# Two edits at the start of an attention and gated-MLP kernel: a limit on loads under way, and wider weights for the first block's projections

## The chip, the cores and the metric

The kernel runs on one core of a Trainium2 chip. The metric is the device time of one execution in microseconds, the median of several runs. TensorE multiplies matrices into PSUM, VectorE (DVE) and ScalarE (ACT) work on elements, GpSimd (POOL) does a few elementwise sums, and SyncE (SP) issues nearly all transfers between HBM and SBUF. PE stands for TensorE's matmuls and PEld for its weight loads.

## The reference

Two stages follow each other. The first is linear attention with random features, for 8 batches, 8 heads, 576 tokens and 64 channels a head:

```python
def phi(x):
    proj = np.einsum('bhsd,md->bhsm', x, omega)      # 64 channels -> 128 features
    sq = np.sum(x * x, axis=-1, keepdims=True) / 2.0
    h = proj - sq
    h = h - np.max(h, axis=-1, keepdims=True)
    return np.exp(h) / np.sqrt(m)
q_p, k_p = phi(q * scale), phi(k * scale)
kv = np.einsum('bhsm,bhsd->bhmd', k_p, v)
out = (q_p @ kv) / (q_p @ k_p.sum(2) + 1e-6)
```

The second takes the result as 4608 tokens of 512 channels and computes `((x @ w_a) * (x @ w_b)) @ w_out` with 1536 inner channels. All is float32.

## The kernel before

**Blocks and pairs.** A block is one batch. Two heads form a pair, their 64 channels each filling 128 partitions, so a block has four pairs (`NHP`). The attention of block 0 runs first; that of later blocks is woven into the MLP of the block before. The MLP splits its float32 operands into two float32r parts and runs three products for each, in `moe_block` (L1307 and the output product L1120) for the first blocks and in a seven-product scheme in `moe_block7` (L1405) for the rest.

**Order.** Every operation is an entry of a graph (`g.op`). The long list `ORDER` fixes in which order they are emitted, so each engine's instructions stand in a fixed order; an engine that waits holds up all that is behind it. Neither the list nor the slots of the buffers are touched by the change.

**Projections.** `four` (L576 and on) projects 512 columns of k and q of a pair: for each of 4 chunks of 128 tokens, 2 halves `t` of 64 tokens and 2 heads `w`, one matmul (L587) with 64 rows by 64 columns of X as weights and the 128 columns of omega streaming. That makes 16 matmuls, each of which shows as two rows of the trace (two passes of float32). The results stand in two PSUM tiles, `ppk` and `ppq`, one for each head row group. After it `scores` takes maxima on DVE (L659), biases (L666 to L673) and the exponentials on ACT (L680). Block 0 calls `four` nine times: twice for each of its four pairs, and once (`Xe`, tiles `ppke` and `ppqe`) for the last 64 tokens of all heads. Later blocks call it too, and `eight` (L607) has the same loop.

**Loads.** The helper `dma` (L406 and L407) issues a transfer on SP's queue. In the order of issue the first thirty are: X in two halves, ident, Xe, X, nat, then from the seventh X, v, nat, X, v, nat, raw (w_out), raw, raw, v, raw, raw, raw (w_out), natee, natk, v, v, X, raw (w_out), raw, natq, raw, natkk, raw. X holds transposed k and q of a pair, nat the same untransposed for the sums of squares (squared on POOL L750 or ACT L566, summed on DVE L752 or L571), v the values, raw weights of the MLP as they come from HBM. `om` (omega) is loaded by ACT's queue. A load takes its place in SBUF from a ring of buffers and waits until the old content is no longer read.

Of the kernel before, what the change touches and what calls it, by code (L numbers as in the profile page):

```python
# [17 lines left out]
P = 128  # L18
B, H, S, D, M = 8, 8, 576, 64, 128
# [177 lines left out]
    at=(  # L197
        "0123456705613412652106537451673260731742751346507163014510110101010101101010100101011010101001010101101001010101010101010101010110101010101010101010101010010101"
        "01010101010101010101010101010101010101010101"),
# [20 lines left out]
    w="345610287a9b",  # L220
    x="01230123012301230110",
    ab="01010101010101010101010101010101010101010101010101011001",
    a="101010101010101010101010",
# [15 lines left out]
    t=(  # L239
        "1230421341023401234102340123401234012340123401234012340123401234012340123401234012340123401234012340123401234012340123401234012340123401234012340123401234012340"  # L240
        "12340123"),
# [3 lines left out]
    c="021021021021021021021021021021021021021021021021021021021021021021021021021021021021",  # L245
# [110 lines left out]
def tile_attention_moe(ctx: ExitStack, tc: tile.TileContext, kqt, kqtt, kqn, kqnt, vx, omst, idn, wab, wout, out):  # L356
    nc = tc.nc
# [7 lines left out]
    def f(ap):  # L365
        return ap.bitcast(F32)

    g = Graph()
    for name, n in dict(X=2, Xw=0, natw=0, nat=2, x2=0, v=2, hk=1, hq=2, qd=1, kvz=0, sm=3, sq=3, ht=3, Xt=1, xl=0, xts=2, rd=2, x=4, xa=2, xf=2, Sa=2, Sb=2, st=0,
                        w=NF, u=NF, t=0, tst=0, wo=3, raw=2, a=2, c=0, bq=0, ghl=2, osb=0, ot=0, owr=0, og=0, ogf=0, oc=0, zs=1, z2=1, zb=2, k2=2, kl=1, dn=1, tails=0, zq=2, zx=2,  # L370
                        at=CFG["AT"], ab=2, o=4).items():
# [31 lines left out]
    def subber(o, i, hi):  # L403
        return lambda e: ENG[e].tensor_tensor(o(), i(), f(hi()), op=ALU.subtract)

    def dma(dst, src):  # L406
        return lambda e: nc.sync.dma_start(dst(), src())  # L407


    ident = fixed([P, P], F32, "ident")  # L410
# [20 lines left out]
    if CFG["IDSP"]:  # L431
        g.op({"SP": 450}, dma(lambda: ident.ap[:], lambda: idn), w=[(ident, None)], prio=-1396.5, nbytes=65536)
    else:
        g.op({"ACT": 60}, lambda e: nc.scalar.dma_start(ident.ap[:], idn), w=[(ident, None)], prio=-5000, nbytes=65536)
# [35 lines left out]
    for n, (kind, i, w) in enumerate(units):  # L470
        pr = 4000 + n * 4000 / len(units)
        more = late[:10] if n < 18 else late[:6] if n < 24 else late[:3] if n < 30 else late[:1] if n < 33 else []
        raw = g.buf("raw", [P, NW], I64 if wide else F32, f"raw{n}", more)
        src = (wab[i, w] if kind == "ab" else wout[i])
        g.op({"SP": 450}, dma(lambda raw=raw: raw.ap[:], lambda src=src: src), w=[(raw, None)], alloc=[raw], prio=pr - 600,
             nbytes=P * NW * (8 if wide else 4))
        if kind == "ab":
            hb = wab_b[i, w] = g.buf("wu"[i % 2], [P, 2, NC4, P], F32R, f"w{'ab'[w]}{i}")
            v = lambda hb, k: hb.ap[:, k].rearrange("p c f -> p (c f)")
        else:  # L480
            hb = wo_b[i] = g.buf("wo", [P, 2, E], F32R, f"wo{i}")
            v = lambda hb, k: hb.ap[:, k]
        convert(raw, lambda hb=hb, v=v: v(hb, 0), lambda hb=hb, v=v: v(hb, 1), hb, NW, pr, CFG["CONV"][0] + n * CFG["CONV"][1], n < NF)
        if kind == "o":
            db = g.buf(None, None, None, f"wod{i}")
            wo_store[i] = db
            g.op({"SP": 450}, dma(lambda i=i: wod[i], lambda hb=hb: f(hb.ap)), r=[(hb, None)], w=[(db, None)], prio=pr + 600,
                 nbytes=P * 2 * E * 4)
# [87 lines left out]
    def four(nm, b, pri, x, xdep, dst, c0, sm, sq, al, deps, mg, more):  # L576

        pps = [g.buf("at", [P, 4 * M], F32, f"pp{'kq'[w]}{nm}{c0}", more) for w in range(2)]
        plain = b == 0 and sq is not None
        mo = om2 if plain else om  # L580

        def go(e):
            for c in range(4):
                for t in range(2):
                    for w in range(2):
                        rows, half = slice(D * w, D * w + D), slice(D * t, D * t + D)
                        nc.tensor.matmul(pps[w].ap[half, c * M:c * M + M], x()[rows, c * P + D * t:c * P + D * t + D], mo.ap[rows], start=True, stop=True)  # L587
        lead = g.op({"PE": 940}, go, r=[*xdep, (mo, None)], w=[(pp, "p") for pp in pps], alloc=[*pps, *al], prio=pri, deps=deps, margin=mg, mode="r")
        flat = [lambda pp=pp: pp.ap for pp in pps]
        scores(nm, b, pri, x, xdep, dst, c0, sm, sq, flat, [[(pp, "p")] for pp in pps], more, plain)  # L590
        return lead
# [1040 lines left out]
```

## Time and profile before

| | |
|---|---|
| median of 3 runs | 1031.1 us (1031.01 to 1032.39) |
| the profiled execution | 1031.69 us |
| its span, first to last instruction | 1029.7 us |
| PE busy | 1021.7 us, 99% of the span, 9963 matmul rows |
| PEld busy | 900.4 us, 87% |
| DVE, ACT, POOL busy | 789.8 us, 637.8 us, 110.8 us |
| DMA | 312.95 MB, 304 GB/s over the span |

Busy time counts each engine's own instructions; a matmul's row includes its way through the array, so rows that follow closely overlap. About 2 us of the profiled execution lie outside the span.

### The profile page before, as it was taken

The numbers are of one execution on the slowest core, as the hardware profiler recorded it, in microseconds if no ns is written. First come the engines' busy times: TensorE is split into PE (matmuls) and PEld (weight loads), VectorE is DVE, ScalarE is ACT, GpSimd is POOL, SyncE is SP. The second block draws the span as 40 slices with busy tenths as digits, with TensorE's granted clock in tenths as the row PEclk, the third lists the DMA queues.
The fourth block names the chain that finished last, engine by engine and source line by source line (L and its number), as shares of the span: only waits on it lengthen the run. The fifth ranks groups of instructions, "written<-read, shape, count | busy, mean of one in ns | idle before, by whom it ended". The sixth has DMA issues, their size and how long they took to land.

```text
span 1029.7 us, 25658 instructions
## 1 busy us (share of the span) xinstructions
PE 1021.7 (99%) x9963; PEld 900.4 (87%) x9963; DVE 789.8 (77%) x1561; ACT 637.8 (62%) x1688; POOL 110.8 (11%) x182
## 2 busy tenths in 40 slices
PE   9999999999999999999999999999999999999998
PEld 7777777778788889888889988888888999999998
DVE  7999999999987877776767767687756467877555
ACT  7999998776676666675666556675654134344322
POOL 2012111210111111111110011111110000000000
PEclk9999999999999999999999999999999999999999
DMA  9787888998999999989898998989797888989981
GB/s 355 244 308 255 274 257 281 328 320 285 338 338 321 340 350 333 341 299 324 286 341 306 325 290 284 350 273 320 242 331 244 307 281 329 366 319 346 358 310 60
DMA packets 122185, 312.95 MB, mean 304 GB/s; under 512 B 17488, under 2 KB 39120, under 8 KB 122064
## 3 DMA queue, kind: packets, MB, share of 16 engines
q1 hardware_dynamic: 121600, 310.72, 87.6%
q8 instruction: 79, 1.29, 0.5%
q10 hardware_dynamic: 464, 0.59, 0.2%
q14 instruction: 42, 0.34, 0.1%
HBM read 254.74 MB, written 56.52 MB: 302 GB/s over the span
## 4 chain that ended last, share of the span: by engine, by line
PE 96%; DVE 3%; ACT 0%; issue 0%; DVEq 0%; ACTq 0%
PE p L1405 41%; PE o L1120 23%; PE pb L1307 6%; PE pa L1307 6%; PE o_P L1190 5%; PE pkv L906 3%; PE pm L977 2%; PE ppk L607 2%; PE ppk L587 2%; PE p L607 1%; PE p L1190 1%; DVE sm L659 1%; PE ppke L587 1%; DVE raw L456 0%; PE none L426 0%; DVE sq L752 0%
## 5 line engine op out<-in xcount | busy, mean ns | idle before, releaser
L1120 PE MATMUL o<-wo,ghl 128*128 128x512 f32 x1008 | 269.6, 397 | 0.0
L1120 PEld LDWEIGHTS o<-wo,ghl 128*128 128x128 f32 x1008 | 178.6, 188 | 35.5 <-issue 4.3
L396 ACT COPY c<-p 128x512 f32<-128x512 f32 x150 | 87.5, 583 | 182.0 <-PE p L1405 174.4
L1417 DVE TENSOR_TENSOR c<-p,c 128x512 f32<-128x512 f32 x144 | 98.7, 685 | 63.8 <-PE p L1405 36.5
L1405 PE MATMUL p<-Sa,t 128*128 128x256 f32 x1008 | 133.9, 282 | 0.0
L1405 PEld LDWEIGHTS p<-Sa,t 128*128 128x128 f32 x1008 | 126.9, 190 | 2.4 <-issue 0.3
L859 POOL TENSOR_TENSOR z<-hk 128x256 f32<-128x256 f32 x54 | 47.2, 873 | 610.5 <-ACT hk L627 356.1
L1481 DVE TENSOR_TENSOR c<-c 128x512 f32<-128x512 f32 x82 | 56.7, 696 | 46.3 <-ACT c L396 45.7
L1307 PE MATMUL pa<-x,wa 128*128 128x512 f32 x288 | 79.6, 400 | 0.0
L941 ACT ACTIVATE hq<-hq,dn 128x128 f32<-128x128 f32 x216 | 70.5, 393 | 11.9 <-DVE dn L937 11.5
L1307 PE MATMUL pb<-x,wb 128*128 128x512 f32 x288 | 77.8, 397 | 0.0
L1405 PE MATMUL p<-x,wb 128*128 128x256 f32 x504 | 73.5, 281 | 0.0
L1405 PE MATMUL p<-x,wa 128*128 128x256 f32 x504 | 73.4, 281 | 0.0
L1405 PEld LDWEIGHTS p<-x,wa 128*128 128x128 f32 x504 | 67.7, 189 | 2.9
L1405 PE MATMUL p<-Sb,bq 128*128 128x256 f32 x504 | 67.7, 283 | 0.0
L1405 PE MATMUL p<-x,t 128*128 128x256 f32 x504 | 67.5, 282 | 0.0
L1405 PEld LDWEIGHTS p<-Sb,bq 128*128 128x128 f32 x504 | 64.9, 189 | 2.9
L1405 PEld LDWEIGHTS p<-x,t 128*128 128x128 f32 x504 | 64.7, 189 | 2.9
L1405 PE MATMUL p<-Sb,t 128*128 128x256 f32 x504 | 67.0, 282 | 0.0
L1405 PEld LDWEIGHTS p<-x,wb 128*128 128x128 f32 x504 | 65.6, 189 | 0.1
L1405 PEld LDWEIGHTS p<-Sb,t 128*128 128x128 f32 x504 | 63.4, 189 | 1.4 <-ACT c L396 0.5
L1307 PEld LDWEIGHTS pb<-x,wb 128*128 128x128 f32 x288 | 53.3, 188 | 12.7 <-issue 0.9
(225 smaller groups left out, 1969.2 us busy)
## 6 DMA issues: line engine op xcount, KB each, us to landing
t<-td SPq DMA_DIRECT2D x168, 512.0 KB
wo<-wod SPq DMA_DIRECT2D x96, 512.0 KB
bq<-bd SPq DMA_DIRECT2D x84, 256.0 KB
qdr<-qd SPq DMA_DIRECT2D x108, 160.0 KB
hq<-qdr SPq DMA_DIRECT2D x27, 640.0 KB
X<-in_kqt_dram SPq DMA_DIRECT2D x30, 512.0 KB
raw<-in_wab_dram SPq DMA_DIRECT2D x24, 512.0 KB
td<-ts SPq DMA_DIRECT2D x24, 512.0 KB
```

What stands on the lines that cost most here:

```text
L396: nc.scalar.copy(o(), i())
L587: nc.tensor.matmul(pps[w].ap[half, c * M:c * M + M], x()[rows, c * P + D * t:c * P + D * t + D], mo.ap[rows], start=True, stop=True)
L607: nc.tensor.matmul(flat[c // 4][w]()[half, c % 4 * M:c % 4 * M + M], x()[rows, c * P + D * t:c * P + D * t + D], om.ap[rows], start=True, ...
L859: g.op({"POOL": pool2(n)}, lambda e: nc.gpsimd.tensor_tensor(o(), a(), c(), op=ALU.add), r=r, w=w, alloc=list(al), prio=pri, deps=zload[-1 ...
L906: nc.tensor.matmul(pkv.ap[D * j + d:D * j + d + Q, 0:M], vb.ap[:, vc, d:d + Q], c(), start=(n == 0), stop=(n == 4))
L941: g.op({"ACT": 392}, lambda e, c=c, src=src: nc.scalar.activation(hq.ap[:, c], src(), AF.Copy, scale=dn.ap[:, c:c + 1]), r=[sd, (dn, None) ...
L1120: nc.tensor.matmul(po.ap[:], ghl.ap[:, gi, t * P:(t + 1) * P], wo.ap[:, wi], start=(n == 0 and i == 0), stop=(n == NF - 1 and i == 2))
L1190: nc.tensor.matmul(pb.ap[:, t], A[0](ai)[:, t * P:(t + 1) * P], W[0](wi), start=begin and t == j == 0, stop=stop and j == 2 and (t == 1 or ...
L1307: nc.tensor.matmul(pb.ap[:], wt.ap[:, wi, c], xs[c].at(xi), start=(c == 0 and i == 0), stop=(c == NC4 - 1 and i == 2))
L1405: nc.tensor.matmul(pb.ap[:, w], W[w][0](wi, c), X[0](xi, c), start=fresh and n == w == 0, stop=n == 5, skip_group_check=True)
L1417: g.op({"DVE": dve(SM)}, lambda e: nc.vector.tensor_tensor(o.ap[:, q], pb.ap[:], C[y[0]].ap[:, y[1]], op=ALU.add), r=[(pb, 0), (pb, 1), (C ...
L1481: g.op({"DVE": dve(SM)}, lambda e, c=C[k]: nc.vector.tensor_tensor(c.ap[:, :, 1], c.ap[:, :, 1], c.ap[:, :, 0], op=ALU.mult), r=part, w=pa ...
```

## The change

The helper keeps a list of the loads it has issued. From the seventh to the thirtieth, each load waits until the third load before it has landed. In `four`, block 0 takes all 128 tokens of a chunk as the weights of one matmul (64 rows by 128 columns) in place of two matmuls with 64 columns each; for other blocks the loop stays. The matmul's output then fills all 128 partitions of its PSUM tile at once.

```diff
+    loads = []
+
     def dma(dst, src):
-        return lambda e: nc.sync.dma_start(dst(), src())
+
+        def go(e):
+            loads.append(nc.sync.dma_start(dst(), src()).ins)
+            n = len(loads) - 1
+            if 6 <= n < 30:
+                tc.add_manual_dep(loads[n], loads[n - 3].name, mybir.DependencyInfo(mybir.DependencyClass.Sync, mybir.DependencyReason.DATA), reason="few transfers at a time")
+        return go
...
             for c in range(4):
-                for t in range(2):
+                for t in range(2) if b else (None,):
                     for w in range(2):
-                        rows, half = slice(D * w, D * w + D), slice(D * t, D * t + D)
-                        nc.tensor.matmul(pps[w].ap[half, c * M:c * M + M], x()[rows, c * P + D * t:c * P + D * t + D], mo.ap[rows], start=True, stop=True)
+                        rows, half = slice(D * w, D * w + D), slice(0, P) if t is None else slice(D * t, D * t + D)
+                        nc.tensor.matmul(pps[w].ap[half, c * M:c * M + M], x()[rows, c * P + half.start:c * P + half.stop], mo.ap[rows], start=True, stop=True)
```

## Rows read from the trace of the kernel before

**Rows 1.** Busy time by stretch: engine busy us (instructions), granted clock, DMA share, GB/s.
```profile
0.00:50.00 50.00, 46.86 (x821) 37.01 (x822) 43.61 (x112) 41.75 (x126) 7.57 (x20) 1.00 0.81 299
50.00:1015.00 965.00, 964.96 (x9063) 853.71 (x9062) 738.48 (x1435) 595.37 (x1562) 103.20 (x162) 1.00 0.90 308
```

**Rows 2.** The same view, 10 to 50 us, with the sum over its stretches.
```profile
10.00:20.00 10.00, 8.84 (x208) 6.90 (x201) 9.83 (x22) 9.54 (x36) 5.35 (x6) 1.00 1.03 404
20.00:30.00 10.00, 9.70 (x224) 8.41 (x221) 9.73 (x32) 9.57 (x34) 0.20 (x1) 1.00 1.04 401
...
sum 40.00, PE 37.66 PEld 30.44 DVE 39.08 ACT 37.51 POOL 6.28; mean PE 9.42 PEld 7.61 DVE 9.77 ACT 9.38 POOL 1.57
```

**Rows 3.** Chain that ended last, 0 to 120 us: start us, us, what.
```profile
10.56 1.28 DVE sme L659 x2
...
27.45 0.59 DVE sqe L571
...
50.34 2.06 PE pb L1307 x9
```

**Rows 4.** Timeline of DVE: start, us, instruction, idle before and releaser.
```profile
3.72 0.69 DVE L643 TENSOR_TENSOR x<-X 128x512 f32<-128x512 f32 x1 [3.72 <-DMA X<-in_kqt_dram]
5.99 0.69 DVE L659 TENSOR_REDUCE sm<-ppq 128x4 f32<-128x512 f32 x1 [1.58 <-PE ppq L587]
...
9.88 0.68 DVE L659 TENSOR_REDUCE sm<-ppk 128x4 f32<-128x512 f32 x1
10.55 0.69 DVE L659 TENSOR_REDUCE sme<-ppke 128x4 f32<-128x512 f32 x1
```

**Rows 5.** Timeline of PE, warm-up and first projections.
```profile
0.78 3.15 PE L426 MATMUL none<-const-bfloat16-1.0 128*128 128x512 bf16 x7 [0.78 <-PEq L1616]
...
4.18 0.42 PE L587 MATMUL ppk<-om,X 64*64 64x128 f32 x1
...
4.39 0.42 PE L587 MATMUL ppk<-om,X 64*64 64x128 f32 x1
...
6.53 0.27 PE L587 MATMUL ppk<-om,X 64*64 64x128 f32 x1
...
6.64 0.27 PE L587 MATMUL ppk<-om,X 64*64 64x128 f32 x1
```

**Rows 6.** Weight loads grouped by line and shape: busy us, mean ns.
```profile
L1405 PEld LDWEIGHTS p<-Sa,t 128*128 128x128 f32 x1008 | 126.9, 190 | 2.4 <-issue 0.3
...
L587 PEld LDWEIGHTS ppk<-om,X 64*64 64x64 f32 x368 | 21.7, 139 | 7.0 <-issue 2.7 <-DMA om<-in_omst_dram 0.9 <-ACT wb L396 0.4
```

**Rows 7.** Timeline of SP, the queue of loads.
```profile
0.75 0.87 SPq L407 DMA_DIRECT2D X<-in_kqt_dram  x2
...
7.61 0.35 SPq L407 DMA_DIRECT2D raw<-in_wout_dram  x1
9.89 1.66 SPq L407 DMA_DIRECT2D raw<-in_wab_dram  x2
...
17.38 0.33 SPq L407 DMA_DIRECT2D natee<-in_kqnt_dram  x1
...
24.62 0.38 SPq L407 DMA_DIRECT2D raw<-in_wab_dram  x1
```

**Rows 8.** Timeline of POOL: the squares that wait for nat.
```profile
10.01 2.04 POOL L750 TENSOR_TENSOR nat<-nat 128x512 f32<-128x512 f32 x2 [4.88 <-DMA nat<-in_kqn_dram]
...
17.43 1.04 POOL L750 TENSOR_TENSOR nat<-nat 128x512 f32<-128x512 f32 x1 [2.42 <-DMA nat<-in_kqn_dram]
```

**Rows 9.** Timelines of ACT and of PE: first readers of late loads.
```profile
26.55 0.75 ACT L566 ACTIVATE natee<-natee 128x512 f32<-128x512 f32 x1
...
28.99 0.80 ACT L566 ACTIVATE natk<-natk 128x512 f32<-128x512 f32 x1
...
32.94 0.69 PE L1040 MATMUL pkv<-v,hk 128*64 128x66 f32 x16
```

**Rows 10.** Who waited for whom on SP, 0 to 45 us: us, times, longest.
```profile
SPq L407 <- DVE sq L571: 9.1, 1, 9.1
```

## The prediction

> **What bounds the kernel now.** I read the busy time by stretch first. From 50 to 1015 us PE is busy 964.96 of 965 us, while in the first 50 us it is busy 46.86 [rows 1]. Both edits act before about 40 us: the nine projections of block 0 and the loads up to the thirtieth. So whatever they do reaches the end only as a shift of the moment at which PE's solid stretch begins, and the shift arrives there undiminished. It is not multiplied either, since the order of each engine is fixed.
>
> Next comes the chain of waits in that first part. It passes from PE's projections to DVE with the maxima of `sme` at 10.56, stays mostly there (the sum `sqe` at 27.45 is one piece), and from 50.34 it is PE alone [rows 3]. DVE is busy 39.08 of the 40 us from 10 to 50, ACT 37.51, PE 37.66 [rows 2]. Hence the first part is bound by DVE, which has 0.92 us of idle time there in all. DVE's dense run begins at 5.99, when the first projection has ended, after 1.58 us of waiting for it [rows 4].
>
> The loads are the third thing to look at. DMA moves 404 and 401 GB/s from 10 to 30 us, its engines busy throughout [rows 2]. SP issues without a long pause until the thirteenth load at 7.61, and the next one only at 9.89; POOL gets the first nat, the sixth load, at 10.01. The same pairing returns at 17.38, where SP issues natee, the twentieth, and at 17.43, where POOL gets the last nat, the twelfth [rows 7, 8]. So today a load waits for the eighth before it: eight are under way, and the queue of transfers never runs dry.
>
> **The projections, part by part.** A call of `four` makes 4 chunks x 2 passes = 8 groups. A group is now four rows (two halves, two heads) that run in four quarters of the array at once. From group to group it takes 4.39 - 4.18 = 0.21 us early on, and 6.64 - 6.53 = 0.11 us later [rows 5]. The same work at twice the speed is the array's clock at its lower level (1.2 GHz), which it has up to about 6.5 us, and then at 2.4 GHz; PE multiplies from 0.78 on, first in seven matmuls of a warm-up [rows 5], and without a long break up to the rise. Because the group's time halves with the clock, it is set by the array and not by how fast instructions are issued.
>
> After the change a group is two rows, one a head, each with 128 columns of weights. The streams stay 128 columns long and the groups stay eight a call. What goes is half of the instructions, 16 x 9 = 144 matmul rows and as many weight loads, and by the argument above these are not what a group waits for. So I expect no gain from them. What can grow is the weight load: 139 ns for 64 columns and 190 ns for 128 [rows 6], some 51 ns more for 64 columns, so about 0.10 us for loading 128. That fits just under a stream of 0.11. The nearest row with 128 columns of weights is the MLP's product: 9 matmuls in 2.06 us are 0.229 each, while 512 columns at 2.4 GHz are 0.213, so each loses 0.016 [rows 3]. I take this 0.016 for each group: 8 x 0.016 = 0.13 a call.
>
> Four calls stand on the path before DVE's work at 10.55 (two halves of the first pair, one of the second, Xe): 4 x 0.13 = 0.5 us, less the 0.07 for which DVE waits there anyway (9.88 + 0.60 = 10.48, a 512-column maximum being issued every 0.6 us) [rows 4]. That makes **+0.45 us at 10.55**. The other five calls (+0.65 us of PE time) stand beside the DVE run, in PE's 2.3 us that are idle from 10 to 50 [rows 2]; without that cover they would be added. The lower end is 0, since a stream is not shortened. The upper end is a load that is not hidden at all, which is the first rival.
>
> **The limit on loads, part by part.** It removes nothing that is waited for: transfers start in the same order, DMA is already full, and a load cannot land earlier because fewer stand behind it. What it adds is a wait on SP. Everything behind it on SP's queue waits too, but that is again loads, in the same order, up to the thirtieth.
>
> The question is whether three loads are enough to keep the transfers dense. A single load of 256 KB, issued at 0.75, reaches DVE at 3.72 [rows 4, 7]: 2.97 us, of which 0.65 are its bytes at 404 GB/s and 2.32 the way there and back. A load of 512 KB needs 1.30 us for its bytes and one of 330 KB 0.84. With the limit, a load lands at the earliest 2.32 us plus its own bytes after the third before it; in a dense queue it lands after the bytes of three.
> - Three of 512 KB: 3.89 dense against 2.32 + 1.30 = 3.62. Nothing is lost.
> - Two of 512 and one of 330 KB, the last of 512: 3.43 against 3.62, a loss of 0.19. This happens at the ninth, the twelfth and the seventeenth load: 0.56 by natee, the twentieth.
> - From natk on (wout, natee, natk: 2.60 against 2.97; then natee, natk, v: 2.14 against 3.16) another 1.0, so that the v, X and weight loads up to the thirtieth come 1.5 to 1.8 us later.
>
> Who notices? natee: the eighteenth load lands when SP goes on at 24.62 with the twenty-sixth, then come 1.30 for w_out and 0.65 for natee, together 26.57. ACT squares natee at 26.55 without a pause before it [rows 7, 9]. So natee has no slack, and behind ACT's square waits `sqe` on DVE, a piece of the chain [rows 3]. natk, then due at 27.2 + 0.9 = 28.1, is read at 28.99, and the fourth v, due at 28.0 + 1.6 = 29.6, at 32.94 [rows 9]: both in time. The last loads find a cover too: SP stood 9.1 us waiting for DVE's `sq` to release a buffer [rows 10], and a delay of 1.8 is swallowed there. So the limit costs **0.5 us through natee**, between 0 (if the first load's way there and back was longer than a later one's by 0.3 us, all triples fit but the last, which nobody notices) and 2.6 to 3.3 (if all 2.97 us are the way there and back, its bytes hidden in them).
>
> **The sum.** The two delays meet on the same path and are not added: where natee is 0.5 late, the chain is already 0.45 late and reads it at 27.0. The later one counts, +0.5 us. From the profiled 1031.69 that gives 1032.2; the profile stands 0.6 over the median of the runs, so in their measure **1031.1 + 0.5 = 1031.6 us**.
>
> **Rivals.**
> - *Wider weights are not hidden.* Two loads of 128 columns for a group run one after the other, or each only after its own head's stream: 0.11 + 0.10 = 0.21 a group, +0.83 a call, +7.5 for nine, and more while the clock is low (about +0.9). PE's 2.3 us of idle time take some. Result 1031.1 + 6 = about 1037. Against it: now four loads stand beside four streams in 0.11. For it: no row here shows 128 columns in half of the rows. The Trainium skill (TensorE: Matmul & The Clock Gate, "Part 3: Packing small matmuls") says that a weight load overlaps running matmuls only where their row groups differ; by it the next chunk's weights would wait for the stream of their own head. The trace speaks against the rule as far as it goes: the MLP's weights go to the same rows as the matmul before, and its 0.229 a matmul leave 0.016 beside a stream of 0.213, no room for a load of 0.10 [rows 3, 6]. Chance 0.08.
> - *The limit starves the transfers.* At the upper end above, natee comes 2.6 to 3.3 late, ACT and DVE stand still, and the end moves to about 1034. It decides from a way there and back of about 2.7 us, where natee's delay passes the 0.5 of the projections by far. For it: transfers under full load may be answered later than the first one was. Against it: the first load's 2.97 contain its own bytes. Chance 0.11, two thirds of it over +0.2%.
> - *Faster.* Half of the instructions let the first projection end sooner, and DVE's idle 0.92 us go. The most that arrival can give is that 0.92, and the first call has 8 groups of 0.21 = 1.7 us of which I cannot see more than 0.5 going. Result 1029.8. Against it: the clock argument. Chance 0.14, about half of it below 1029.0.
>
> **How the numbers follow.** A measurement of this kernel tells 0.2%, about 2.1 us, from no change: faster is under 1029.0 and slower over 1033.2. The forecast has 0.67, all within. Faster: 0.07. Slower: 0.08 + 0.07 + 0.01 of the forecast's tail = 0.16. Same: 0.77. The range that leaves out 2 in 10 at most goes from 1029.8 to 1034.2; it leaves out the weights that are not hidden and the greater part of the gains.
>
> **What would show it.** In the trace after: matmul rows of the projections 64 by 128, in pairs, 0.11 to 0.13 us apart once the clock is up (0.21 would be the first rival); DVE's first maximum at 6.0 to 6.2 and `sme` at about 11.0; SP's issues from 5.9 us on, each at the landing of the third before; GB/s from 10 to 30 us at 385 to 400 (under 360 is the second rival); ACT idle before natee by up to half a microsecond; PE solid from 50 us on as now. I am wrong if `sme` starts before 10.4, or if a wait for a load other than nat and natee appears on ACT, DVE or PE.

## The result, and the profile after

| | median us | runs | ratio to before, 95% |
|---|---|---|---|
| before | 1031.13 (1030.96 to 1032.39) | 6 | |
| after | 1036.89 (1035.88 to 1038.61) | 6 | 1.0054 [1.0043, 1.0064] |

The change makes the kernel 5.8 us slower, where I had 1031.6 us and no measurable difference as the likeliest case. The profiled execution took 1035.88 us (span 1034.0), 4.2 more than that of before.

Busy time by stretch, after (engine busy us and instructions, granted clock, DMA share, GB/s), answering to [rows 1, 2]:

```profile
10.00:20.00 10.00, 9.44 (x168) 7.97 (x167) 9.86 (x21) 9.54 (x37) 3.84 (x6) 1.00 0.87 288
20.00:30.00 10.00, 7.84 (x132) 6.47 (x128) 7.82 (x23) 6.54 (x23) 0.72 (x2) 1.00 0.92 302
...
0.00:50.00 50.00, 43.06 (x631) 34.66 (x631) 39.59 (x102) 37.35 (x114) 7.59 (x20) 1.00 0.84 278
50.00:1015.00 965.00, 964.87 (x9073) 852.72 (x9072) 741.82 (x1440) 598.71 (x1571) 103.99 (x162) 1.00 0.90 309
```

From 50 us on PE is as solid as before (964.87 of 965). All that was lost was lost earlier: DVE is busy 39.59 us of the first 50 in place of 43.61, and the transfers fell from 404 and 401 to 288 and 302 GB/s.

Timelines of DVE, ACT and PE, after, answering to [rows 4, 5, 9]:

```profile
6.18 0.69 DVE L667 TENSOR_REDUCE sm<-ppq 128x4 f32<-128x512 f32 x1 [1.67 <-PE ppq L595]
...
10.59 0.68 DVE L667 TENSOR_REDUCE sme<-ppke 128x4 f32<-128x512 f32 x1
...
31.96 0.69 DVE L579 TENSOR_REDUCE sqe<-natee 128x8 f32<-128x512 f32 x1 [3.91 <-ACT natee L574]
```
```profile
31.30 0.63 ACT L574 ACTIVATE natee<-natee 128x512 f32<-128x512 f32 x1 [3.85 <-DMA natee<-in_kqnt_dram]
```
```profile
6.60 0.27 PE L595 MATMUL ppk<-om,X 64*128 64x128 f32 x1
6.61 0.27 PE L595 MATMUL ppq<-om,X 64*128 64x128 f32 x1
6.71 0.27 PE L595 MATMUL ppk<-om,X 64*128 64x128 f32 x1
6.72 0.27 PE L595 MATMUL ppq<-om,X 64*128 64x128 f32 x1
```

The pairs of the wide projections are 0.11 us apart, as the groups of four rows were; `sme` starts at 10.59 (before 10.55). So up to 10.6 us nothing is lost. Then ACT stands 3.85 us before natee, and DVE 3.91 us behind it: `sqe` comes at 31.96, 4.5 us later than in the chain of before.

Chain of work that ended last, after, 0 to 60 us (start us, us, what), answering to [rows 3]:

```profile
11.52 4.87 DMA v<-in_vx_dram
16.40 5.44 DMA raw<-in_wab_dram
21.86 4.54 DMA raw<-in_wab_dram
26.41 4.87 DMA natee<-in_kqnt_dram
31.30 0.64 ACT natee L574
31.96 0.69 DVE sqe L579
...
37.52 5.38 DMA natq<-in_kqn_dram
...
43.30 7.12 DMA raw<-in_wab_dram
...
55.00 2.06 PE pb L1315 x9
```

Before, this stretch was DVE's. Now it is, up to natee, a chain of loads, each issued when the third before it has landed, at steps of 4.5 to 5.4 us; the prediction had 3.6 for a 512 KB load, 3.2 for a v and 3.0 for natee. After `sqe` most of it is DVE's again, then come natq and the thirty-first load, which no longer falls under the limit. `pb`, where PE's solid part begins, moved from 50.34 to 55.00, by 4.66 us: nearly all of it, 4.51, was already there at `sqe`.

### The profile page after: what moved, and what is told of

It reads as the page before. It is cut to its first block, busy times and chain, and to the rows that moved or that the text cites. A ratio compares the mean times of both kernels' runs of the same rounds, so it can differ in the third digit from the quotient of the medians.

```text
span 1034.0 us, 25373 instructions
## 1 busy us (share of the span) xinstructions
PE 1022.0 (99%) x9819; PEld 901.3 (87%) x9819; DVE 790.7 (76%) x1561; ACT 638.2 (62%) x1688; POOL 111.6 (11%) x182
## 4 chain that ended last, share of the span: by engine, by line
PE 94%; DMA 4%; DVE 1%; ACT 0%; SPq 0%; issue 0%; ACTq 0%
PE p L1413 41%; PE o L1128 23%; PE pb L1315 6%; PE pa L1315 6%; PE o_P L1198 5%; PE pkv L914 3%; PE pm L985 2%; PE ppk L615 2%; DMA raw<-in_wab_dram 2%; PE p L615 1%; PE ppk L595 1%; PE p L1198 1%; DMA v<-in_vx_dram 1%; PE ppke L595 1%; DMA natq<-in_kqn_dram 1%; DMA X<-in_kqt_dram 0%
```

## The experiments

**Which edit.** The limit alone, with the narrow projections as before:
```
-                for t in range(2) if b else (None,):
+                for t in range(2):
...
```


> The limit of three loads alone, block 0's projections as before. Theory A (the limit starves the transfers, the wider weights cost nothing): 1036.5 +- 1 us, DVE waits 3 to 5 us for natee's square near 27 to 32 us, 285 to 305 GB/s from 10 to 30 us. Theory B (the wider weights cost most of the 5.6 us): 1031 to 1032.5 us.

And the wide projections alone:
```
-            if 6 <= n < 30:
+            if False:
```


> Weights of 64 rows by 128 columns alone, no limit on loads. Theory A: 1030.5 to 1031.7 us, groups of the projections still 0.11 us apart at the higher clock, 400 GB/s from 10 to 30 us. Theory B: 1035 to 1037 us.

Limit alone: 1037.74 us, ratio 1.0055 [1.0043, 1.0068]. Wide projections alone: 1031.24, ratio 0.9996 [0.9988, 1.0005]. The loss belongs to the limit, and no cost of the wide weights can be measured. The same stretches, of the limit alone and then of the wide projections alone:

```profile
10.00:20.00 10.00, 8.87 (x230) 7.17 (x221) 9.78 (x20) 8.42 (x33) 3.44 (x4) 1.00 0.89 294
20.00:30.00 10.00, 7.95 (x174) 6.43 (x168) 8.02 (x24) 6.83 (x24) 2.12 (x4) 1.00 0.90 307
30.00:40.00 10.00, 6.77 (x110) 6.48 (x112) 5.99 (x19) 6.60 (x21) 0.00 (x0) 0.66 0.88 279
```
```profile
10.00:20.00 10.00, 9.34 (x167) 8.00 (x167) 9.82 (x22) 9.61 (x38) 5.36 (x6) 1.00 1.03 403
20.00:30.00 10.00, 9.69 (x183) 8.40 (x179) 9.70 (x33) 9.70 (x35) 0.20 (x1) 1.00 1.03 401
```

The GB/s, the last column, go with the limit, not with the projections.

**How many loads are enough.** The whole change with four, and later with six, in place of three:
```
-                tc.add_manual_dep(loads[n], loads[n - 3].name, ...
+                tc.add_manual_dep(loads[n], loads[n - 4].name, ...
```


> Both edits, but four loads under way in place of three. Theory A with a step of 4.6 to 5.9 us from a load to the third after it, as the trace of the changed kernel shows: four loads of 512 KB need 5.2 us when dense, so nearly dense again; natee lands 0 to 1.5 us late and the time is 1031 to 1033 us. If each load's way there and back were simply longer whatever is under way (over 6 us for the fourth), it stays above 1034 us.

> Both edits, but six loads under way in place of three. Depth theory (a load of 512 KB needs more company than three to keep the 16 DMA engines fed; at eight 1.28 us a load, at four 1.29 to 1.37, at three 1.66): 395 GB/s or more in 10:20 and in 20:30, natee on ACT waited for at most 0.6 us, ratio to before 1.000 (0.9988 to 1.0010). Rival, that every issue that waits for a landing costs by itself, whatever the depth: 22 of the 24 still wait, so a ratio near the 1.0016 of four, and natee still some us late.

Four: 1032.96 us, ratio 1.0016 [1.0007, 1.0025]. Six: 1031.18, ratio 1.0000 [0.9990, 1.0009]. In the profiled execution of four natee still landed 4.0 us later than before, where I had expected 1.5 at most, and was waited for 3.9 us; that execution, 1034.71, was the slowest of its ten. With six, 20 of the 24 loads (the seventh to the twenty-sixth) still go out within 0.1 us of the landing of the sixth before them and nothing is lost, so it is not the waiting of an issue that costs, but how little is under way. The stretches of four, then of six:

```profile
10.00:20.00 10.00, 9.60 (x187) 8.43 (x186) 9.83 (x24) 9.58 (x37) 3.64 (x5) 1.00 0.93 330
20.00:30.00 10.00, 7.24 (x112) 5.87 (x108) 7.07 (x21) 6.33 (x22) 1.24 (x2) 1.00 0.85 304
```
```profile
10.00:20.00 10.00, 9.37 (x182) 8.14 (x183) 9.83 (x24) 9.55 (x36) 4.68 (x6) 1.00 1.04 408
20.00:30.00 10.00, 9.70 (x160) 8.36 (x156) 9.73 (x31) 9.88 (x36) 0.20 (x1) 1.00 1.03 401
```

**Is it natee's place.** The whole change, but natee and natk issued right after the third nat, ahead of six loads of weights (their two operations, 471 and 474, moved up in the written order, behind 415):
```
-... 311 415 271 ...  316 471 329 ...  322 474 323 ...
+... 311 415 471 474 271 ...  316 329 ...  322 323 ...
```


> Both edits, three loads under way, but natee and natk are issued ahead of the six weight loads (as the thirteenth and fourteenth load). Theory A1 (natee's lateness is all that is paid for): DVE's wait of 3.9 us goes and the time is 1031.5 to 1033 us. Theory A2 (all loads are late by 5 us or more, and the next reader takes natee's place: the fourth v, read at 32.94 before and landing at 34.2 under the limit, then the weights that ACT converts near 40 us): 1034 to 1036.5 us, with a wait for a v or raw load or for what they hold up between 30 and 52 us.

1035.57 us, ratio 1.0042 [1.0029, 1.0055]: within the noise of the whole change's 1.0054. The wait for natee is gone and others took its place. Waits from 25 to 50 us (who waited for whom: us, times, longest; line numbers shifted by the shorter list):

```profile
ACT natq L557 <- DMA natq<-in_kqn_dram: 1.6, 1, 1.6
DVE sq L562 <- ACT natq L557: 1.4, 1, 1.4
...
PE pkv L1031 <- DMA v<-in_vx_dram: 1.0, 1, 1.0
```

All loads are late, and the next ones to be read are waited for in natee's place.

**Where along the limit.** The limit of three on the first six of its loads only, and on the other 18 only:
```
-            if 6 <= n < 30:
+            if 6 <= n < 12:      # the other kernel: if 12 <= n < 30:
```


> The limit of three on the seventh to the twelfth load alone, with the wide weights. In the changed kernel the twelfth load ended only 0.4 us later than before (16.38 against 16.01), natee, the twenty-first, 4.8. Theory that the loss builds up from the thirteenth load on: 380 GB/s or more in 20:30, natee waited for at most 1 us, ratio 1.000 to 1.001. Rival, that the loss comes of the engines falling out of step at the first waits, and what follows only carries it on: natee 2 us late or more, ratio 1.002 to 1.005.

> The limit of three on the thirteenth to the thirtieth load alone, with the wide weights. Theory that the loss builds up from the thirteenth load on: nearly all of the change's cost, ratio 1.0035 to 1.006, natee waited for 3 to 5 us on ACT, about 400 GB/s in 5:15 and near 300 in 20:30. Rival (loss from the first waits): ratio under 1.002.

(That expectation counted `om` on ACT's queue too: its "twelfth" is the eleventh of SP's loads, and natee is the twentieth.) First part: 1033.42 us, ratio 1.0017 [1.0007, 1.0027], natee waited for 1.9 us. Second part: 1034.46, ratio 1.0031 [1.0018, 1.0043], natee waited for 2.6 us. Both of my theories missed: neither part carries it all. 1.7 and 3.1 thousandths add up to 4.8, near the whole change's 5.4. Up to natee the first part limits six loads and the second eight. In the profiled executions natee landed 2.9 us later than before with the first part and 2.5 us later with the second, that is 0.5 and 0.3 us for each limited load that natee has to follow. With the first part alone the DMA is full again from 20 us on, and the lateness stays:

```profile
10.00:20.00 10.00, 9.58 (x183) 8.36 (x181) 9.83 (x24) 9.81 (x37) 2.79 (x4) 1.00 0.89 308
20.00:30.00 10.00, 7.48 (x120) 6.11 (x114) 7.94 (x20) 6.96 (x24) 2.01 (x4) 1.00 1.03 407
```

**The loads by themselves.** Attention and MLP left out, the output zeros: loads of 512 KB alone, one, three, four and eight under way; then the same beside 2000 small matmuls, whose instructions also have to be fetched. Each of the four kernels of loads alone ran once:
```
phases = ((1, 6), (3, 15), (4, 16), (8, 24))
...
t = sp.tile([P, 512], wab.dtype, ...)
loads.append(nc.sync.dma_start(t[:], wab[n % NF, n // NF % 2]).ins)
if n:
    tc.add_manual_dep(loads[n], loads[n - (depth if k >= depth else k + 1)].name, ...
```


> The attention and the MLP are left out: loads of 512 KB alone, issued by SP in four stretches with at most 1, 3, 4 and 8 under way (6, 15, 16 and 24 loads). Theory T1 (the way there and back alone makes the step of 5 us): with three under way the step from a load to the third after it is 4.5 us or more here too, 340 GB/s or less. Theory T2 (the way there and back is 2.3 us as the first load of the kernel had it, and the rest comes from what other work does to single DMA engines, above all the reading of PE's instructions): one at a time takes 3.6 us a load, three run dense at 3.9 us a step and 395 to 410 GB/s, like eight.

> The same loads beside a stream of 2000 small matmuls on zeros, which makes PE read its instructions through the DMA engines all the time; the rest is left out. T2: with three under way the step grows by 0.5 to 1.5 us over that without the matmuls, with eight by far less. T1: no difference between the two at any depth beyond 0.2 us a step.

Loads alone, the four phases in turn (the columns before the clock are DVE and POOL, idle):

```profile
4.00:22.00 18.00, 0.00 (x0) 0.00 (x0) 1.00 0.48 146
30.00:48.00 18.00, 0.00 (x0) 0.00 (x0) 1.00 0.87 315
55.00:71.00 16.00, 0.00 (x0) 0.00 (x0) 1.00 0.99 396
75.00:104.00 29.00, 0.00 (x0) 0.00 (x0) 1.00 1.03 411
```

One load at a time takes 3.5 us from landing to landing: 1.28 of bytes and 2.25 of the way there and back, which is what the prediction had read (2.32). Three at a time should then take 3.84 for three, being more than 3.53. They take 1.66 us a load, 4.98 for three (4.4 to 5.9 from a load to the third after it), where four need 1.31 a load and eight 1.28. The matmuls change nothing for three (1.66 again) and a little for four (1.37) and eight (1.30). So fetched instructions are not the cause with three: the whole loss is there without them. With four there is a difference: the first steps from a load to the fourth after it were 7.25 and 6.75 us in place of 5.1. How much of the 0.16% that four cost in the kernel comes of that was not tested.

**What it depends on.** Loads alone again, with other sizes and numbers under way:
```
phases = ((3, 2, 9), (2, 2, 8), (6, 0, 24), (3, 0, 15))   # depth; 2: 1 MB, 0: 256 KB in 64 rows; loads
```


> Loads alone; attention and MLP are left out, and the output is zeros. Phases, one after the other: 9 loads of 1 MB three at a time, 8 of 1 MB two at a time, 24 of 256 KB (64 rows) six at a time, 15 of 256 KB three at a time. Theory that bytes under way decide (1.5 MB gave 316 GB/s, 2 MB 400): three of 1 MB 400 GB/s or more, two of 1 MB about 400, six of 256 KB about 316, three of 256 KB below 220. Rival, that the number of loads decides (three always leave engines idle for a fixed share): three of 1 MB about 316, six of 256 KB 400 or more, two of 1 MB below 300.

and always three, of 256, 384, 640, 768, 512 KB, and 512 KB from two queues:
```
phases = ((3, 1, 256, 15), (3, 1, 384, 15), (3, 2, 320, 15), (3, 2, 384, 15), (3, 1, 512, 15), (3, 0, 512, 15))
```


> Loads alone, always three under way; attention and MLP are left out, and the output is zeros. Phases of 15 loads, one after the other: 256, 384, 640, 768 and 512 KB (all 128 rows) from SP's queue, then 512 KB in turn from SP's and ACT's queue. Theory A (fixed way of 2.25 us and 410 GB/s, the sum of the prediction): us a load 0.96, 1.07, 1.60, 1.92, 1.28, 1.28. Theory B (the way of a load among others is longer, 3.7 us beside its bytes, as the mean step of 4.98 in the loads-alone run has it): 1.45, 1.55, 1.77, 1.92, 1.66, and 1.66 for two queues. If one queue's handling is the cause, the last phase is below 1.45.

The first of these, by phase:

```profile
5.00:26.00 21.00, 0.00 (x0) 0.00 (x0) 1.00 1.00 403
33.00:49.00 16.00, 0.00 (x0) 0.00 (x0) 1.00 1.00 393
57.00:82.00 25.00, 0.00 (x0) 0.00 (x0) 1.00 1.03 199
88.00:101.00 13.00, 0.00 (x0) 0.00 (x0) 1.00 0.89 201
```

Two loads of 1 MB keep the DMA as full as four of 512 KB, so it is not the number of loads that decides. The two phases of 64 rows can't be read as I meant: with six under way the DMA is busy 1.03 at 199 GB/s, and a packet to 64 rows takes twice as long (0.33 us against 0.16). They say something else: three of these loads were nearly as fast as six (1.33 against 1.30 us a load), although each takes about as long as one of 512 KB to all rows, where three lose a quarter.

The second, by phase:

```profile
5.00:18.00 13.00, 0.00 (x0) 0.00 (x0) 1.00 0.74 239
24.00:40.00 16.00, 0.00 (x0) 0.00 (x0) 1.00 0.86 281
48.00:71.00 23.00, 0.00 (x0) 0.00 (x0) 1.00 0.91 321
80.00:105.00 25.00, 0.00 (x0) 0.00 (x0) 1.00 0.96 363
112.00:131.00 19.00, 0.00 (x0) 0.00 (x0) 1.00 0.88 312
138.00:159.00 21.00, 0.00 (x0) 0.00 (x0) 1.00 0.89 321
```

From landing to landing that is 1.12, 1.36, 1.99, 2.12, 1.65 and, with two queues, 1.81 us a load. The sum of the prediction gives 0.96, 1.07, 1.60, 1.92, 1.28, 1.28; my other theory 1.45, 1.55, 1.77, 1.92, 1.66, 1.66. Neither fits: the first is short by 0.16 to 0.53 everywhere, the second is too high for small loads and too low for large. A second queue does not help (the 321 GB/s of its stretch count stores of the output that begin at 154 us; without the two loads beside them it is 1.78 us a load). Three loads fall short of 411 GB/s at every size from 256 to 768 KB, and the share lost shrinks as the bytes under way grow.

The landings of the 16 DMA engines show how, though not why. A load counts as landed when its last engine has finished. In the first run of loads alone, with one, four or eight under way, the first and the last of the 16 are 0.3 to 0.7 us apart (0.8 at the very first load), with three 1.1 to 2.1. With three some packets take up to 1.18 us, where the median is 0.16; with one, the first packets of a load do too (up to 1.17), and with eight in full flow the longest was 0.18. Idle engines and slow packets both count: the DMA share was 0.87 with three and 1.03 with eight, the mean packet 0.18 and 0.16 us. The next load is issued after the last of the engines; that the others have run dry by then fits these numbers, but the trace does not say which engine carried a packet. The spread by itself costs nothing: in the kernel before, from the sixth load to the twenty-seventh, the first and the last landing are 2.4 to 3.2 us apart, at some 400 GB/s with eight under way.

## Why the prediction was wrong

**What bounds the kernel: right for a delay at natee.** Both edits act only in the first 50 us, and the delay at natee arrives nearly undiminished: 4.5 us at `sqe`, 4.7 at `pb`, 4.3 at the end of the span. That an earlier shift arrives undiminished too, as the prediction had it for its 0.45 us at `sme`, does not hold: with the wide projections alone an X load landed 1.3 us later than before and `sme` started at 11.25, 0.70 later, but `sqe` stood at 27.58 and `pb` at 50.48, 0.13 and 0.14 later.

**The projections: right in kind, too dear.** I charged 0.016 us a group, +0.45 at `sme`. The groups came 0.111 to 0.112 us apart where they had been 0.109, and `sme` was 0.04 later, in an execution whose first X came 0.09 later. The first rival (1037 us by weights that are not hidden) came close to the measured time and is nevertheless wrong: the wide projections alone gave 0.9996. The weight load of a 64 by 128 product does run beside the stream of its own rows. Weight loads, after:

```profile
6.50 0.19 PEld L595 LDWEIGHTS ppk<-om,X 64*128 64x128 f32 x1
6.50 0.19 PEld L595 LDWEIGHTS ppq<-om,X 64*128 64x128 f32 x1
6.61 0.19 PEld L595 LDWEIGHTS ppk<-om,X 64*128 64x128 f32 x1
6.61 0.19 PEld L595 LDWEIGHTS ppq<-om,X 64*128 64x128 f32 x1
```

The loads at 6.61 begin while the matmuls of 6.60 and 6.61 are only starting, and the next pair follows at 6.71. The Trainium skill's sentence that the load overlaps only where row groups differ (TensorE: Matmul & The Clock Gate, "Part 3: Packing small matmuls") does not hold for this pair, at 0.11 us from pair to pair.

**The limit: the step that failed** is "Three of 512 KB: 3.89 dense against 2.32 + 1.30 = 3.62. Nothing is lost." The 2.32 was right for a lone load (2.25 measured). It was wrong to use it as the way of a load that has two others beside it: the step measured 4.98 with loads alone, 3.8 to 6.4 in the kernel, for most 4.5 to 5.9, and the 0.27 us that seemed to be spare were no spare at all. As the kernel before never had three under way, no row of it could show this; the lone load was taken as exact where it was a lower bound.

The Trainium skill gives the access time of HBM as 0.2 us, and 2 us at high load, and makes it the chief part of a transfer's fixed cost (DMA: Bandwidth & Descriptors, "Latency and other measured facts"). The direction agrees with the loads of 512 KB, where the way beside the bytes went from 2.25 us alone to 3.7 among three; but two loads of 1 MB, at the higher rate of 393 GB/s, had 2.5 to 3.2, so the rate does not decide it. What the engines were waiting for in that time no run shows.

**Who notices: the right place, the wrong size.** natee has no slack, and `sqe` stands behind ACT's square: both seen. The delay was not 0.5 us but 4.8: natee landed at 31.28, where it was 26.50. Up to natee fourteen loads are limited, so that is 0.34 us for each. My second rival named this mechanism with 0.11, but its upper end (2.6 to 3.3 us late) came from the same lone load with its bytes counted in, which is no bound for a load among others. That the later loads had cover was said for a delay of 1.5 to 1.8 us (2.1 at the twenty-eighth and after, by the prediction's own rule). It was 9.6 for natq (42.91 against 33.29), and that was too much: with natee moved out of the way, natq and v were waited for.

**A term that I did not have: the clock.** 4.2 of the 5.8 us are in the two profiled executions. Of the other 1.6, 0.6 is that the profiled execution of before stood that far above its median, and 1.0 that the profiled one of after stood below its own. That of after was the fastest of its six and the only one with a mean granted clock of 1.000; the others, 1036.6 to 1038.6 us, have 0.996 to 0.998. What lies behind such a number the limit alone shows. There PE stood 4.31 us before `pkv` (3.30 in the profiled execution of after, whose clock stayed up), and the granted clock fell between 30 and 32 us to its lower level, 1.2 GHz, where it stayed over 32 to 36 us:

```profile
28.00:30.00 2.00, 0.92 (x32) 0.78 (x28) 0.25 (x1) 0.00 (x0) 0.00 (x0) 1.00 1.01 395
30.00:32.00 2.00, 0.00 (x0) 0.00 (x0) 0.00 (x0) 0.00 (x0) 0.00 (x0) 0.74 0.76 223
32.00:34.00 2.00, 0.77 (x14) 0.77 (x16) 0.89 (x2) 1.55 (x6) 0.00 (x0) 0.50 0.69 183
34.00:36.00 2.00, 2.00 (x34) 1.88 (x31) 1.93 (x11) 1.75 (x6) 0.00 (x0) 0.50 0.97 354
36.00:38.00 2.00, 2.00 (x12) 2.00 (x11) 1.50 (x3) 1.74 (x7) 0.00 (x0) 0.55 1.06 313
```

That execution took 1038.98 us, 3.1 more than the profiled one of after; natee, which landed 1.15 later there, accounts for about 1 of them, so about 2 are left, which I put down to the clock; that is an estimate. That the same happened in the other five executions of after is an inference from their mean clocks, since they have no trace.

**Still open** is what makes some packets slow (with one load under way they are the first after an idle moment), and so why 0.3 us of spare in the sum do not protect three loads of 512 KB while 0.3 us (5.12 against 2.25 + 2.56) do nearly protect two of 1 MB (5.30 measured) and three loads to 64 rows lose next to nothing.

## What to carry to other kernels

The way there and back of one lone transfer is a lower bound for a transfer among others; before fewer are kept under way, measure the step at that very number. On this kernel three loads of 512 KB lost about a quarter of the rate, four nearly nothing when alone but still 0.16% of the kernel, and six nothing. And a wait early in a kernel that is solid afterwards can cost its full length, as natee's did, or little, as the 0.70 us at `sme` did with the wide projections alone: look for the place with no slack behind it. If TensorE's clock falls during the wait, as it did with the limit alone, more is lost.

## What the runs showed of the hardware

- The rate of loads of 512 KB with one, three, four and eight under way was 146, 315, 396 and 411 GB/s; two of 1 MB gave 393.
- Loads to 64 of the 128 rows moved at 199 GB/s with the DMA engines fully busy (six under way).
- Loads alternating between SP's and ACT's queue, three under way, were no faster than from one queue (1.78 to 1.81 against 1.65 us a load).
- A 64 by 128 weight load ran beside the matmul on the same rows; pairs went through at 0.11 us, as four of 64 by 64 did.
